# Sink attention with a mixer: the products of two heads beside each other in halves of the TensorE array, and a written order ahead of the branch

## The chip, the cores and the metric

The kernel runs on one core of a Trainium2 chip. The metric is the time of one execution on the device in microseconds (us). The kernel before is given as a median of 3 executions; the profile shows a further execution of it.

## What is computed

Inputs have 4 batches, 8 heads, 768 positions and 64 numbers per head. Attention keeps, for each query, 4 sink keys and a window of the last 128 keys. A low-rank mixer over positions (rank 32) and a two-layer network with a hidden width of 2048 follow, each with a residual sum.

```python
scores = scale * np.matmul(q, k.transpose(0, 1, 3, 2))
keep = is_sink | in_window
scores = np.where(keep, scores, -1000000000.0)
a = np.exp(scores - np.max(scores, axis=-1, keepdims=True))
a = a / (np.sum(a, axis=-1, keepdims=True) + 1e-09)
attn = np.matmul(a, v)                # then x: [4, 768, 512]
h = x.transpose(0, 2, 1) @ U @ V
u = x + h.transpose(0, 2, 1)
out = u + np.maximum(u @ w_ch1, 0.0) @ w_ch2
```

U, V and the two weight matrices arrive as 8-byte floats.

## The kernel before, in words

**Attention.** One head and one half of its queries (three blocks of 128) are a unit. For each block, TensorE makes the scores against 4 sink keys and at most 256 window keys in one bank (line 637 or, in split form, lines 640 and 641). VectorE adds the mask and takes the minimum of the negated scores in one instruction with a second one that reads its accumulator (643). ScalarE makes the exponentials and their sums (648). The unit is then normalised (667 to 691), transposed on TensorE (702), masked into triangles (711 on VectorE, 727 on GpSimd), and multiplied with the values (752); a copy puts the result into `xT`. Batches 0 and 1 (`WHOLE`) do the scores and values in plain 4-byte floats; batches 2 and 3 split each operand into two parts first. A score contracts over 64 numbers: in batches 0 and 1 the lower 64 of the 128 partitions of `q` and `k` hold zeros, which come with the inputs (and from four memsets for the first two heads, lines 1287 and 1288). A value product of batches 0 and 1 has 128 output rows, of which the lower 64 belong to the next block's values and are not used.

**Weights.** Each of the 16 steps of the network (`f`) needs two pieces of 128x512 weights. A piece in 8-byte floats is loaded into `big`, turned into a 4-byte float by the VectorE and ScalarE steps of lines 94 to 103, and split into two parts (lines 462, 469). These are the conversions; there are 32 of them, all in the first third of the execution. Converted weights also go to memory (`wd`) and are fetched from there later.

**Network.** A step on TensorE is 12 products of 384 columns (966 to 968), a ReLU (974) and its remainder `hl` (977), and 9 products of 512 columns (987). Batch 0 runs the 16 steps on both halves of the positions in groups of four: four new steps on one half, the same four on the other, and so on. Attention of batch `b + 1` is placed among the network steps of batch `b`.

**Order.** No loop order is written out. Every operation is a `Step` with a duration, an engine or a choice of engines, and a due time. `Plan.order` places them by these numbers and their dependences, several rounds forwards and backwards, and the program is emitted in the resulting order. So a change of one duration or dependence moves instructions everywhere. Each engine then runs its own instructions strictly in that order and waits at each for what it needs. Ahead of the network and attention stands a short part that loads two limits, builds masks and branches on them (`Masks`, `load_scalars`, lines 1271 to 1303).

## Time and profile before

| what | us |
|---|---|
| median of 3 executions (761.8 to 762.37) | 762.2 |
| the profiled execution | 760.85 |
| its span, first to last instruction | 759.1 |
| TensorE busy | 745.9 (98%) |
| VectorE busy | 459.1 (60%) |
| ScalarE busy | 353.4 (47%) |
| GpSimd busy | 187.9 (25%) |

The span does not hold 1.75 us that lie around it. A record of a matmul in the profile is longer than the time until the next one starts, because the array works on several at once; the busy share of TensorE can therefore stay near 100% while it still has room. A plain 4-byte product stands in the profile as two records.

### The profile page before, as it was taken

To read this page: it belongs to the slowest core of one execution; us is meant where nothing else is said; L and a number is where in the kernel's file an instruction comes from. 1 tells how busy PE (TensorE), PEld (TensorE's weight loads), DVE (VectorE), ACT (ScalarE), POOL (GpSimd) and SP (SyncE) were. 2 spreads that over 40 slices of the span, in tenths; PEclk is the share of its full clock that TensorE was granted. 3 is DMA by queue.
4 is the path that set the end of the run, shared out by engine and by line. 5 is a ranking of instruction groups with operands and counts; after the bars stand their busy time and mean duration, and the time that the engine had idled before them with its cause. 6 is when DMAs were issued, how large, how long until landed. Compare 5 with 4: busy or idle time off the path is not lost.

```text
span 759.1 us, 11690 instructions
## 1 busy us (share of the span) xinstructions
PE 745.9 (98%) x4012; PEld 667.4 (88%) x4012; DVE 459.1 (60%) x1184; ACT 353.4 (47%) x1024; POOL 187.9 (25%) x288
## 2 busy tenths in 40 slices
PE   8999999999999999999999999999999999999997
PEld 6786998888888999999999989899999898989995
DVE  8989779898899586676853176766653131112111
ACT  6997367666676374564551155555542111111110
POOL 4761011223232344424611033522501000000000
PEclk9999999999999999999999999999999999999999
DMA  8898477773876478762586448761266527523752
GB/s 289 277 318 293 180 268 251 264 260 105 280 236 232 147 192 259 232 220 77 168 265 218 166 130 280 233 191 49 69 217 225 210 92 260 186 102 129 257 189 95
DMA packets 46981, 153.90 MB, mean 203 GB/s; under 512 B 5824, under 2 KB 13888, under 8 KB 37440
## 3 DMA queue, kind: packets, MB, share of 16 engines
q1 hardware_dynamic: 46752, 152.86, 60.7%
q8 instruction: 33, 0.54, 0.3%
q14 instruction: 36, 0.29, 0.1%
q10 hardware_dynamic: 160, 0.20, 0.1%
HBM read 123.42 MB, written 29.62 MB: 202 GB/s over the span
## 4 chain that ended last, share of the span: by engine, by line
PE 91%; DVE 5%; ACT 2%; issue 1%; POOL 0%; DMA 0%; POOLq 0%; DVEq 0%
PE bank L987 35%; PE bank L966 12%; PE bank L968 12%; PE bank L967 12%; PE bank L752 6%; PE bank L637 4%; PE bank L702 2%; PE bank L640 2%; PE bank L641 1%; PE bank L866 1%; DVE bank L101 1%; PE bank L1004 1%; ACT p L648 1%; DVE p L469 1%; PE bank L849 1%
## 5 line engine op out<-in xcount | busy, mean ns | idle before, releaser
L987 PE MATMUL bank<-w,hh 128*128 128x512 f32 x768 | 243.4, 398 | 0.0
L977 DVE SCALAR_TENSOR_TENSOR hl<-bank,hh 128x384 fp32r<-128x384 f32 x128 | 70.8, 553 | 189.2 <-ACT hh L974 188.7
L966 PE MATMUL bank<-ul,w 128*128 128x384 f32 x512 | 178.9, 349 | 0.0
L968 PE MATMUL bank<-uh,w 128*128 128x384 f32 x512 | 172.8, 337 | 0.0
L967 PE MATMUL bank<-uh,w 128*128 128x384 f32 x512 | 172.3, 337 | 0.0
L974 ACT ACTIVATE hh<-bank 128x384 fp32r<-128x384 f32 x119 | 58.4, 491 | 220.8 <-PE bank L968 219.9
L987 PEld LDWEIGHTS bank<-w,hh 128*128 128x128 f32 x768 | 139.3, 188 | 19.4
L987 PE MATMUL bank<-w,hl 128*128 128x512 f32 x384 | 152.3, 397 | 0.0
L648 ACT ACTIVATE p<-p,mn 128x260 f32<-128x260 f32 (+1 forms) x192 | 93.3, 487 | 41.0 <-DVE mn L643 40.5
L967 PEld LDWEIGHTS bank<-uh,w 128*128 128x128 f32 x512 | 96.4, 188 | 5.7
L966 PEld LDWEIGHTS bank<-ul,w 128*128 128x128 f32 x512 | 96.2, 188 | 5.7
L968 PEld LDWEIGHTS bank<-uh,w 128*128 128x128 f32 x512 | 96.0, 188 | 0.0
L987 PEld LDWEIGHTS bank<-w,hl 128*128 128x128 f32 x384 | 72.1, 188 | 17.7 <-DVE hl L977 1.1
L643 DVE CUSTOM_DVE_ANT_0 p<-bank,mask 128x260 f32<-128x260 f32 (+1 forms) x192 | 70.9, 400 | 17.6 <-PE bank L641 13.3
L682 POOL TENSOR_TENSOR p<-p,r 128x396 f32<-128x396 f32 x33 | 29.0, 878 | 113.1 <-DVE r L670 95.9
L471 POOL TENSOR_TENSOR ul<-xT,uh 128x384 fp32r<-128x384 f32 x15 | 15.1, 1022 | 122.0 <-ACT uh L462 84.8
L727 POOL TENSOR_SCALAR_AFFINE_SELECT oph<-oph 128x384 f32<-128x384 f32 (+1 forms) x64 | 36.3, 567 | 21.5 <-ACT oph L462 17.7
L471 POOL TENSOR_TENSOR p<-p 128x256 f32<-128x256 f32 (+1 forms) x22 | 19.2, 871 | 81.2 <-ACT p L648 77.7
L752 PEld LDWEIGHTS bank<-oph,vhl 128*128 128x128 f32 x224 | 35.8, 190 | 3.9 <-POOL oph L727 0.6
L752 PE MATMUL bank<-oph,vhl 128*128 128x256 f32 (+1 forms) x224 | 38.9, 303 | 0.0
L648 ACT ACTIVATION_READ_ACCUMULATOR p<-p,mn 128x1 f32 x192 | 36.1, 188 | 0.0
L702 PE MATMUL bank<-ident,p 128*128 128x128 f32 x192 | 33.3, 277 | 1.9 <-ACT p L680 1.5
(178 smaller groups left out, 1079.5 us busy)
## 6 DMA issues: line engine op xcount, KB each, us to landing
w<-wd SPq DMA_DIRECT2D x60, 1024.0 KB, 4.9
big<-in_w_dram SPq DMA_DIRECT2D x32, 512.0 KB, 5.4
wd<-w SPq DMA_DIRECT2D x14, 1024.0 KB, 4.8
big<-xd SPq DMA_DIRECT2D x33, 256.0 KB, 3.1
qkraw<-in_q_dram SPq DMA_DIRECT2D x39, 192.0 KB, 4.3
qkraw<-in_k_dram SPq DMA_DIRECT2D x32, 198.0 KB, 5.6
out_dram<-big SPq DMA_DIRECT2D x24, 256.0 KB, 2.1
v_raw<-in_v_dram SPq DMA_DIRECT2D x16, 192.0 KB, 2.8
```

What stands on the lines that cost most here:

```text
L471: ways["POOL"] = (gps(n), lambda: nc.gpsimd.tensor_tensor(dst(), a(), b(), op), True)
L643: add("DVE", dve(wd), lambda st=st, u=u, lo=lo, wd=wd, qb=qb: nc.vector.tensor_tensor_reduce(p()[:, u, NS + lo:], st()[:, :wd], self.mask[ ...
L648: add("ACT", act(wd) + 0.22, lambda u=u, lo=lo: nc.scalar.activation(p()[:, u, NS + lo:], p()[:, u, NS + lo:], AF.Exp, bias=mn()[:, u:u + ...
L702: nc.tensor.transpose(tr()[:, u * P:(u + 1) * P], p()[:, u, SW + NS:], self.ident)
L727: add("POOL", 0.126 + CH * 0.914e-3, lambda t=t: nc.gpsimd.affine_select(as_(t()[:, :, 1, :]), f32(t()[:, :, 1, :]), [[0, NBLK], [1, P]], ...
L752: nc.tensor.matmul(out, st, f32(mv) if whole else mv, start=part == 0 and i == 0, stop=part == len(t) - 1 and i == len(mms) - 1, skip_grou ...
L966: nc.tensor.matmul(ph()[:, :CH], wh, ul()[:, d, :], start=d == 0, stop=False)
L967: nc.tensor.matmul(ph()[:, :CH], wl, uh()[:, d, :], start=False, stop=False)
L968: nc.tensor.matmul(ph()[:, :CH], wh, uh()[:, d, :], start=False, stop=d == NC - 1)
L974: self.plan.any({"ACT": (act(CH), lambda: nc.scalar.activation(hh(), ph()[:, :CH], AF.Relu)), "DVE": (dve(CH), lambda: nc.vector.tensor_sc ...
L977: add("DVE", dve(CH), lambda: nc.vector.scalar_tensor_tensor(hl(), ph()[:, :CH], 0.0, f32(hh()), ALU.max, ALU.subtract), r=(ph, hh), w=(hl ...
L987: nc.tensor.matmul(acc[k](), a()[:, sl], w()[:, m, :], start=not begin and i == 0 and j == 0, stop=i == n - 1 and j == 2)
```

## The change

In batches 0 and 1, two heads are now one unit. `load_pair` puts the two heads' `q` and `k` into the upper and the lower 64 partitions of one tile, without zeros. For every block of queries, `attend_pair` issues two score products, one per head, on the two halves of the partitions and into two banks. For the values it issues the two heads' products in turn, each with 64 stationary columns, into the upper and the lower 64 rows of one bank, and one copy of 128x384 replaces two of 64x384. The planner's durations for these are `0.105 + wd / 600.0` for two scores of `wd` columns (before `0.005 + wd / 600.0` for one) and 1.25 and 1.50 for two heads' values (before 1.08 and 1.30 for one). A second tile per unit for the exponentials is taken from the ring `qkraw`. Sums and minima share one small tile. The batches 2 and 3 keep their form. The part ahead of the branch is emitted as written, with the distances of `Masks` first and the masks filled ahead of the load of the flag.

```diff
+NSM = 7
+PAIRED = 2
...
-ACC = (0xFFFF, 0xFFFF, 0xFFFF, 0xFFFF)
-WHOLE = {0: (0xFFFF, 0xFFFF), 1: (0xFF, 0xFF)}
...
+def two_heads(x, b, pr):
+
+    return x[b, 2 * pr:2 * pr + 2].rearrange("h d n -> (h d) n")
...
-        kr, qr = (self.kh(), self.qs()) if h % 2 else (self.kl(), self.qkraw())
-        self.put(kr, lambda: (f32(kr()[:, :k1 - k0]), self.k[b, h][:, k0:k1]), (k1 - k0) * 512, t0 - 16)
-        self.put(qr, lambda: (f32(qr()[:, :q1 - q0]), self.q[b, h][:, q0:q1]), (q1 - q0) * 512, t0 - 15)
-        return qr, kr, None, q0, k0
-
-    def scores(self, half, t0, acc, qs, kh, kl, qbase=0, kbase=0):
+        kr, qr = self.kh(), self.qs()
+        self.put(kr, lambda: (f32(kr()[:, :k1 - k0]), two_heads(self.k, b, pr)[:, k0:k1]), (k1 - k0) * 512, t0 - 16)
+        self.put(qr, lambda: (f32(qr()[:, :q1 - q0]), two_heads(self.q, b, pr)[:, q0:q1]), (q1 - q0) * 512, t0 - 15)
+        return qr, kr, q0, k0
+
+    def load_v_pair(self, b, pr, blocks, t0):
+
+        k0, k1 = blocks
+        n = k1 - k0
+        t = self.vhl()
+        flat = lambda: f32(t().rearrange("p n s d -> p (n s d)")[:, :2 * n * D])
+        for i in range(2):
+            self.put(t, lambda i=i: (flat()[:, i * n * D:(i + 1) * n * D].rearrange("p (n d) -> p n d", n=n),
+                                     self.v[b, 2 * pr + i][:, k0:k1, :]), n * 32768, t0 - 8, part=i)
+        return t, flat, k0, n
...
+    def attend_pair(self, b, pr, half, t0, qk, v, xT):
+
         nc, add = self.nc, self.plan.add
-        p, mn, sm = self.p(), self.mn(), self.sm()
+        qr, kr, qbase, kbase = qk
+        wide = lambda: self.pool.tile([P, NB * SW], F32, name="qkraw", bufs=NRAW).rearrange("p (n s) -> p n s", n=NBLK)
+        ps = [self.p(), self.qkraw(wide)]
+        sms = [self.ms(), self.ms()]
+        for u in range(NBLK):
+            qb = half * NBLK + u
+            lo = P if qb == 0 else 0
+            k0 = max(qb - 1, 0) * SW + (NS if qb else 0) - kbase
+            q0 = qb * P - qbase
+            wd = UW - lo
+            sts = [self.bank(), self.bank()]
+
+            def mms(sts=sts, q0=q0, k0=k0, wd=wd):
+                for i, st in enumerate(sts):
+                    rows = slice(i * D, (i + 1) * D)
+                    nc.tensor.matmul(
+                        st()[:, :wd], f32(qr()[rows, q0:q0 + P]), f32(kr()[rows, k0:k0 + wd]), start=True, stop=True)
+            add("PE", 0.105 + wd / 600.0, mms, r=[qr, kr] + [(p, u) for p in ps], w=sts, prio=t0, after=self.gate)
+            for st, p, sm in zip(sts, ps, sms):
+                self.soften(st, p, sm, u, lo, wd, qb, t0)
+        ts = []
+        for i in range(2):
+            self.normalise(b, 2 * pr + i, half, t0 + i, ps[i], sms[i], self.sinks[b])
+            ts += self.transposes(half, t0 + i, ps[i], True, self.opl if i else self.oph)
+        pa = self.bank()
+        t, flat, kb0, n = v
+        mms = []
+        for kb in range(max(half * NBLK - 1, 0), (half + 1) * NBLK):
+            lo = 2 * (kb - half * NBLK) + 1
+            hi = min(lo + 2, 2 * NBLK)
+            lo = max(lo, 0)
+            mms.append((kb, lo, hi, max(kb - half * NBLK, 0)))
+
+        def run():
+            for j, (kb, lo, hi, c0) in enumerate(mms):
+                for i in range(2):
+                    mv = ts[i]().rearrange("p u s j -> p (u s j)")[:, lo * P:hi * P]
+                    at = (i * n + kb - kb0) * D
+                    nc.tensor.matmul(
+                        pa()[i * D:(i + 1) * D, c0 * P:(c0 + hi - lo) * P], flat()[:, at:at + D], f32(mv),
+                        start=j == 0, stop=j == len(mms) - 1, skip_group_check=True)
+        both = [(xT, (half, 0)), (xT, (half, 1))]
+        add("PE", (0.0, 1.25, 1.50)[len(mms) - 2], run, r=ts + [t] + both, w=(pa,), prio=t0)
+        self.copy(CH, lambda: xT()[:, half * CH:(half + 1) * CH], lambda: pa()[:, :CH], psum=True, r=(pa,), w=both, prio=t0)
+
...
+            if b < PAIRED:
+                if h % 2 == 0:
+                    pr = h // 2
+                    qk, v = self.load_pair(b, pr, (0, 1), t0), self.load_v_pair(b, pr, (0, NB), t0)
+                    for half in range(2):
+                        self.attend_pair(b, pr, half, self.t0(16 * b + 2 * (h + half)), qk, v, self.x[b][-1])
+                continue
+            qk = self.prep_qk(b, h, (0, 1), t0)
+            v = self.prep_v(b, h, (0, NB), t0)
             for half in range(2):
-                self.attend(b, h, half, self.t0(16 * b + 2 * h + half), qk, v, self.x[b][-1], whole_v)
+                self.attend(b, h, half, self.t0(16 * b + 2 * h + half), qk, v, self.x[b][-1])
...
+        for pr in range(NPAIR):
+            t0 = self.t0(16 * b + half * H + 2 * pr)
+            qk = self.load_pair(b, pr, (half, half), t0)
+            v = self.load_v_pair(b, pr, (max(half * NBLK - 1, 0), (half + 1) * NBLK), t0)
+            self.attend_pair(b, pr, half, t0, qk, v, self.x[b][pr])
...
-        self.mn, self.sm = ring(NP + 1, [P, NBLK], F32, "mn"), ring(NP + 1, [P, NBLK], F32, "sm")
-        self.rr = ring(3, [P, NBLK], F32, "r")
+        self.ms = ring(NSM, [P, 2 * NBLK], F32, "ms")
+        self.rr = ring(4, [P, NBLK], F32, "r")
...
+    with tc.tile_pool(name="work", bufs=1) as work, tc.tile_pool(name="idle", bufs=1, space=PSUM) as idle, \
+            tc.manual_schedule():
...
+        masks = Masks(nc, sp, work)
         first = []
-        for h, n in enumerate((HALF, DM)):
-            qt, kt = (pre.tile([P, n], F32, name=f"first{h}{x}") for x in "qk")
-            nc.sync.dma_start(kt[0:D, :NBLK * SW], k[0, h][0:D, :NBLK * SW])
-            nc.scalar.dma_start(qt[0:D, :CH], q[0, h][0:D, :CH])
-            nc.vector.memset(qt[D:P, :CH], 0.0)
-            nc.vector.memset(kt[D:P, :NBLK * SW], 0.0)
+        for pr, n in enumerate((HALF, DM)):
+            qt, kt = (pre.tile([P, n], F32, name=f"first{pr}{x}") for x in "qk")
+            nc.sync.dma_start(kt[:, :NBLK * SW], two_heads(k, 0, pr)[:, :NBLK * SW])
+            nc.scalar.dma_start(qt[:, :CH], two_heads(q, 0, pr)[:, :CH])
             first.append((qt, kt))
...
         ns, w, flag = values()
+        masks.fill(ns, w)
         rv = nc.values_load(flag[0:1, 0:1], min_val=0, max_val=1)
-        masks.fill(ns, w)
```

On TensorE, at the start of attention of batch 0, this stands in the program before (`first`, `kl`, `kh` are keys, `qkraw`, `qs` queries, `p` exponentials, `oph`, `opl` their transposes, `vhl` values):

```order
L637 MATMUL bank_165<-kh,qs 128x132
L637 MATMUL bank_166<-kh,qs 128x260
L637 MATMUL bank_167<-kh,qs 128x260
L702 MATMUL bank_168<-ident,p_179 128x128 x3
L752 MATMUL bank_169<-oph,vhl 128x256 x2
L752 MATMUL bank_169<-oph,vhl 128x128
```

And this in the changed program:

```order
L652 MATMUL bank_166<-kh,qs 128x132
L652 MATMUL bank_167<-kh,qs 128x132
L652 MATMUL bank_168<-kh,qs 128x260
L652 MATMUL bank_169<-kh,qs 128x260
L652 MATMUL bank_162<-kh,qs 128x260
L652 MATMUL bank_163<-kh,qs 128x260
L745 MATMUL bank_164<-ident,p_177 128x128 x3
L745 MATMUL bank_165<-ident,qkraw 128x128 x3
L675 MATMUL bank_166<-oph,vhl 64x256
L675 MATMUL bank_166<-opl,vhl 64x256
```

The number of products per head is the same; they now come in twos, from `oph` and `opl` in turn for the values.

On TensorE, where the first attention of batch 1 stands among the network steps of batch 0 (`w`, `ul`, `uh` belong to the network), before:

```order
L968 MATMUL bank_167<-uh,w_173 128x384
L637 MATMUL bank_168<-kl,qkraw 128x132
L637 MATMUL bank_164<-kl,qkraw 128x260
L637 MATMUL bank_166<-kl,qkraw 128x260
L637 MATMUL bank_163<-kl,qkraw 128x260
L637 MATMUL bank_168<-kl,qkraw 128x260
L637 MATMUL bank_164<-kl,qkraw 128x260
L966 MATMUL bank_167<-ul,w_173 128x384
```

And in the changed program:

```order
L1008 MATMUL bank_167<-uh,w_172 128x384
L652 MATMUL bank_169<-kh,qs 128x132
L652 MATMUL bank_168<-kh,qs 128x132
L652 MATMUL bank_166<-kh,qs 128x260
L652 MATMUL bank_162<-kh,qs 128x260
L1006 MATMUL bank_167<-ul,w_172 128x384
L1007 MATMUL bank_167<-uh,w_172 128x384
L1008 MATMUL bank_167<-uh,w_172 128x384
L652 MATMUL bank_169<-kh,qs 128x260
L652 MATMUL bank_168<-kh,qs 128x260
L1006 MATMUL bank_167<-ul,w_172 128x384
```

The twelve scores of a pair of heads are now spread in smaller groups. Between the start of the network of batch 0 and the end of attention of batch 1, the changed program has 17 groups of scores and 8 of values, each with network products or transposes ahead of it and behind it.

On VectorE, around the first remainder `hl` of the network, before (`bank`, `nr` and `w` belong to conversions; a row that writes `w` ends one):

```order
L469 TENSOR_TENSOR w_174<-bank_163,w_174 128x512
L101 SCALAR_TENSOR_TENSOR bank_164<-big_93,nr 128x512
L96 TENSOR_SCALAR nr<-nr 128x512
L102 TENSOR_TENSOR bank_164<-nr,bank_164 128x512
L942 TENSOR_TENSOR xT<-xT,bank_168 128x384
...
L469 TENSOR_TENSOR w_174<-bank_164,w_174 128x512
...
L977 SCALAR_TENSOR_TENSOR hl<-bank_165,hh 128x384
```

And in the changed program:

```order
L474 TENSOR_TENSOR w_170<-bank_167,w_170 128x512
L101 TENSOR_SCALAR nr<-nr 128x512
L106 SCALAR_TENSOR_TENSOR bank_164<-big_107,nr 128x512
L982 TENSOR_TENSOR xT<-xT,bank_165 128x384
...
L474 TENSOR_TENSOR w_172<-bank_164,w_172 128x512
L104 SCALAR_TENSOR_TENSOR nr<-big_109,nr 128x512
L1017 SCALAR_TENSOR_TENSOR hl<-bank_168,hh 128x384
```

Ahead of the first `hl`, the program before ends six conversions (`w_171`, `w_173` and `w_174`, two each), the changed one three (two of `w_170`, one of `w_172`). The other three now stand behind it.

## Rows read from the trace of the kernel before

**Rows 1.** The page: busy share in tenths, 40 slices of 19 us.

```profile
PE   8999999999999999999999999999999999999997
...
DVE  8989779898899586676853176766653131112111
ACT  6997367666676374564551155555542111111110
```

**Rows 2.** Stretches; length, busy time of each engine (instructions), granted clock, DMA share.

```profile
core 0: us, PE busy (x) PEld busy (x) DVE busy (x) ACT busy (x) POOL busy (x), PEclk, DMA share, GB/s
3.40:79.70 76.30, 71.55 (x367) 57.33 (x367) 70.77 (x237) 62.75 (x207) 36.36 (x54) 1.00 0.90 307
79.70:248.00 168.30, 167.00 (x879) 148.55 (x878) 145.21 (x364) 105.64 (x279) 37.35 (x44) 1.00 0.69 230
...
14.80:31.80 17.00, 16.97 (x95) 14.61 (x96) 15.63 (x64) 16.90 (x68) 12.17 (x19) 1.00 0.88 274
...
262.00:753.50 491.50, 490.82 (x2689) 446.09 (x2687) 232.76 (x566) 179.63 (x530) 106.56 (x172) 1.00 0.55 180
```

**Rows 3.** The chain that ended last, 0 to 90 us: start, length.

```profile
16.17 1.10 PE bank L637 x6
...
60.81 0.20 DVE nr L96
61.01 0.62 DVE bank L101
61.65 0.69 DVE bank L102
...
62.54 0.61 DVE nr L99
63.17 0.29 DVE nr L100
63.46 0.60 DVE w L469
...
76.56 0.18 PE bank L966
...
80.80 2.09 PE bank L987 x9
```

**Rows 4.** VectorE in order of time, the first and a later remainder of the network.

```profile
79.69 0.55 DVE L977 SCALAR_TENSOR_TENSOR hl<-bank,hh 128x384 fp32r<-128x384 f32 x1
...
247.98 0.56 DVE L977 SCALAR_TENSOR_TENSOR hl<-bank,hh 128x384 fp32r<-128x384 f32 x1 [0.26 <-ACT hh L974]
```

**Rows 5.** The chain that ended last, 85 to 260 us.

```profile
101.62 2.42 PE bank L637 x12
...
125.79 2.39 PE bank L752 x14
...
219.74 1.84 DVE nr L96
```

**Rows 6.** TensorE in order of time, 196 us.

```profile
195.88 0.34 PE L968 MATMUL bank<-uh,w 128*128 128x384 f32 x1
196.06 0.34 PE L966 MATMUL bank<-ul,w 128*128 128x384 f32 x1
```

**Rows 7.** ScalarE by line and form, 5 to 76 us; count, busy us, mean ns.

```profile
L462 ACT COPY xT<-bank 64x384 f32<-64x384 f32 x14 | 6.6, 468 | 0.2
```

**Rows 8.** All engines in order of time, the start.

```profile
3.42 0.16 DVE L116 SCALAR_TENSOR_TENSOR sc_t<-sc_raw 128x2 f32<-128x2 int32 x1 [0.85 <-DMA sc_raw<-in_limits_dram]
...
4.20 0.29 DVE L145 CAST m_back<-m_rel 128x268 f32<-128x268 int32 x1
...
5.28 2.51 PE L637 MATMUL bank<-first0k,first0q 128*128 128x132 f32 x6 [0.68 <-DVE m_ck L155]
...
6.57 0.29 DVE L643 CUSTOM_DVE_ANT_0 p<-bank,mask 128x132 f32<-128x132 f32 x1 [0.27 <-DVE mask L160]
```

More of the change, by code (lines that the diff above doesn't have):

```diff
@@ L626, in scores @@
+    def scores(self, half, t0, qs, kh, kl, qbase=0, kbase=0):
+        nc, add = self.nc, self.plan.add
+        p, sm = self.p(), self.ms()
         for u in range(NBLK):
@@ L671, in normalise @@
         kept = lambda: p()[:, :, SW:]
         by = lambda: r().unsqueeze(2).broadcast_to([P, NBLK, SW])
-        if acc:
-            u0 = 1 if half == 0 else 0
-            own, past = lambda: p()[:, u0:, SW + NS:], lambda: p()[:, u0:, NS:SW]
-            self.tt((NBLK - u0) * P, own, own, past, ALU.add, w=(p,), prio=t0)
-            def scale():
-                for u in range(NBLK):
-                    nc.scalar.activation(p()[:, u, SW:], p()[:, u, SW:], AF.Copy, scale=r()[:, u:u + 1])
-            self.plan.any({"ACT": (NBLK * 0.3, scale),
-                           "POOL": (0.82, lambda: nc.gpsimd.tensor_tensor(kept(), kept(), by(), ALU.mult), True),
-                           "DVE": (dve(NBLK * SW), lambda: nc.vector.tensor_tensor(kept(), kept(), by(), ALU.mult), True)},
-                          r=(r,), w=(p,), prio=t0)
-        else:
-            self.plan.any({"POOL": (0.82, lambda: nc.gpsimd.tensor_tensor(kept(), kept(), by(), ALU.mult), True),
-                           "DVE": (dve(NBLK * SW), lambda: nc.vector.tensor_tensor(kept(), kept(), by(), ALU.mult), True)},
-                          r=(r,), w=(p,), prio=t0)
+        u0 = 1 if half == 0 else 0
@@ new lines, in normalise, with scale @@
+        own, past = lambda: p()[:, u0:, SW + NS:], lambda: p()[:, u0:, NS:SW]
+        self.tt((NBLK - u0) * P, own, own, past, ALU.add, w=(p,), prio=t0)
+        def scale():
+            for u in range(NBLK):
+                nc.scalar.activation(p()[:, u, SW:], p()[:, u, SW:], AF.Copy, scale=r()[:, u:u + 1])
+        self.plan.any({"ACT": (NBLK * 0.3, scale),
+                       "POOL": (0.82, lambda: nc.gpsimd.tensor_tensor(kept(), kept(), by(), ALU.mult), True),
+                       "DVE": (dve(NBLK * SW), lambda: nc.vector.tensor_tensor(kept(), kept(), by(), ALU.mult), True)},
+                      r=(r,), w=(p,), prio=t0)
@@ L693, in normalise, with transposes @@
                       r=(p,), w=((psink, (half, h)),), prio=t0)
-    def transposes(self, half, t0, p, whole):
+    def transposes(self, half, t0, p, whole, own=None):
         nc, add = self.nc, self.plan.add
         tr = self.bank()
-        res = [self.oph()] if whole else [self.oph(), self.opl()]
+        res = [own()] if whole else [self.oph(), self.opl()]
         def mms():
@@ L764, in values, with attend @@
                 r=(pa, tb), w=((xT, (half, hh)),), prio=t0)
-    def attend(self, b, h, half, t0, qk, v, xT, whole=False):
-        acc = ACC[b] >> (half * H + h) & 1
-        p, sm = self.scores(half, t0, acc, *qk)
-        self.normalise(b, h, half, t0, acc, p, sm, self.sinks[b])
-        t = self.transposes(half, t0, p, whole)
-        self.values(h, half, t0, t, v, xT)
+    def attend(self, b, h, half, t0, qk, v, xT):
+        p, sm = self.scores(half, t0, *qk)
+        self.normalise(b, h, half, t0, p, sm, self.sinks[b])
+        self.values(h, half, t0, self.transposes(half, t0, p, False), v, xT)
     def attention(self, b):
@@ L1119, in run @@
             tiles.append(self.pool.tile([P, NBLK, SW + SW], F32, name=f"p{i}"))
-            nc.gpsimd.memset(tiles[-1][:, :, 0:NS], 0.0)
         with tc.manual_schedule():
@@ L1273, in sink_attention_mixer @@
     ident = sp.tile([P, P], F32, name="ident")
-    with tc.tile_pool(name="work", bufs=1) as work, tc.tile_pool(name="idle", bufs=1, space=PSUM) as idle:
+    with tc.tile_pool(name="work", bufs=1) as work, tc.tile_pool(name="idle", bufs=1, space=PSUM) as idle, \
+            tc.manual_schedule():
         zero = nc.const_aps.tensor(0.0, [P, P], F32)
@@ L1293, in sink_attention_mixer @@
             nc.sync.dma_start(early[-1].bitcast(U16)[:, 1:4 * n + 1], src)
-        masks = Masks(nc, sp, work)
         tri = sp.tile([P, 2, P], F32, name="tri")
```

100 lines of the change are left out of this document (32 added, 68 removed).

## The prediction

> **What bounds the kernel now.** I read the slices of the page first. TensorE is at 8 or 9 tenths throughout, VectorE at 8 and 9 in the first third and then falls to 1 [rows 1]. So I cut the span into stretches [rows 2], at two instructions of VectorE: the first remainder `hl` of the network, at 79.7 us, and the one at 248.0 us that stands just ahead of the end of attention of batch 1 [rows 4]. I call 3.4 to 79.7 us stage A (attention of batch 0), 79.7 to 248 us stage B (network of batch 0, attention of batch 1, most conversions), and what follows stage C.
>
> In stage A VectorE is busy 70.8 of 76.3 us, 92.8%, and between 14.8 and 31.8 us ScalarE 16.9 of 17.0 us [rows 2]. The chain passes through TensorE's scores for a while (16.17 us) and then through conversions on VectorE (from 60.81 us) [rows 3]: three engines take turns as the last one. In stage B TensorE is busy 167.0 of 168.3 us and VectorE 145.2, 86.3% [rows 2]; the chain is TensorE's, apart from a piece near 220 us where an instruction of a conversion took 1.84 us [rows 5] that took 0.20 us at 60.81 us [rows 3]. Stage C is TensorE alone: 490.8 of 491.5 us from 262 to 753.5 us, VectorE under half [rows 2]. The change leaves that work as it is, so what is won ahead of 248 us is kept to the end, and nothing can be won behind it.
>
> **The parts of the change, and what each costs.**
>
> *The start.* VectorE begins the distances at 4.20 us, behind the limits (3.42 us), and its first score at 6.57 us [rows 8]. In the changed order the distances stand ahead of the limits, in time that the four removed memsets and a wait filled. The chain of the limits to the flag stays. TensorE's first score at 5.28 us [rows 8] cannot come earlier, since it needs the flag. What is freed is the stretch from 4.20 us to the filling of the masks, about 1 us, of which the arrival of the scores takes some back: I take -0.5 us, bounds -1 and 0.
>
> *Loads.* A pair's `q` and `k` need as many bytes as one padded head did, so these loads are halved. The DMA share of stage A is 0.90 [rows 2], but the chain there is of engines, not of transfers [rows 3]: nothing is taken for this. If the cover were gone, the transfers would be fewer than now, so the sign is safe. SP's order puts the weights' loads behind fewer loads of heads.
>
> *Copies.* 14 copies of 64x384 to `xT` on ScalarE in stage A took 0.468 us each [rows 7]. A pair needs one copy instead of two, so of 16 copies 8 go, 3.7 us on ScalarE or VectorE. Beside them the merged small tiles and the dropped memsets cost nothing that shows.
>
> *Conversions that move.* One conversion on VectorE is, in the chain, 0.20 + 0.62 + 0.69 + 0.61 + 0.29 + 0.60 = 3.0 us [rows 3]. The changed order has three of them ahead of the first `hl`, the present one six. So 9.0 us of VectorE's work leave stage A and enter stage B. In stage A this shortens the engine that is last at its end: -9.0 us. It could be more, by the copies (-13), if TensorE's freed time lets the engines pack; it could be less (-5), if ScalarE, full from 14.8 us on, keeps the attention at its length and only the end of the stage gets shorter.
>
> *The first weights come later.* The network now starts with one and a half steps' weights. Behind the first `hl`, the other two and a half of the first four steps are five conversions, 15.0 us, with three more `hl` of 0.55 us [rows 4]: 16.6 us of VectorE. In that time TensorE has six half steps of 2.1 us (80.80 us, 9 products of 512 columns, and as much for the 12 of 384 columns between 76.56 us and there, twice over) [rows 3], 12.6 us. TensorE then waits about 4 us that it does not wait now. Queued behind it are all network steps of batch 0.
>
> *TensorE's pairs, in stage B.* One head costs 2.42 us for its six scores (12 records) and 2.39 us for its seven value products [rows 5]; eight heads 38.5 us. No row shows two products in two parts of the array: all rows of before use 128 by 128. Bounds: if they run fully beside each other, 19.3 us remain. A product is two records, so the second head's first record starts beside the first head's second; each group of pairs then ends one record late, 2.42 / 12 to 0.22 us. With 25 groups (17 of scores, 8 of values) that is 5.5 us, 24.8 us in all, 13.7 saved. At the other end a product ends 0.34 us after its start while the next starts after 0.18 us [rows 6]: if the array has to run empty at each of 50 switches, 0.16 to 0.17 us each, 8.5 us more are lost and 5.2 saved. I take 12 us, near the first: in stage B transposes, scores and network products alternate now, and TensorE's busy time has no hole from it (167.0 of 168.3 us [rows 2]). In stage A the same saving does not count by itself, since VectorE and ScalarE are full there.
>
> The Trainium skill speaks against this part: its page "TensorEngine Tiling (Array Packing)", section "Tiling Modes", says that a change of the tiling mode drains TensorE. By that the lower saving, 5.2 us, would hold, and the sum below would be 750 us and not 748. No run of before shows a change of mode.
>
> *Stage B, taken together.* TensorE would need 167.0 - 12 + 4 = 159.0 us. VectorE would be busy 145.2 + 9.0 = 154.2 us, 97% of that. It has not been that full over any long stretch: 92.8% in stage A, 86.3% in B [rows 2]. So TensorE's saving runs into VectorE. I take 94%, a little over stage A because its waits for TensorE's scores get rarer: 164.0 us, -4.3 us. Bounds: 159.0 us (-9.3), and, with the share of today, 178.7 us (+10.4).
>
> **The sum.** 760.85 (the profiled execution) - 0.5 - 9.0 - 4.3 = 747.05 us. The median lies 1.35 us above that execution, so 748.4 us.
>
> **Rivals.**
>
> *TensorE alone bounds stage B.* VectorE packs to 97%, for which its choices of engine speak (ScalarE is busy 105.6 of 168.3 us there [rows 2]): -9.3 instead of -4.3 us, 743.4 us; with the copies in stage A 739.4 us.
>
> *VectorE is as full as now and no fuller.* Every conversion waits for loads, ScalarE and banks as before, and the work that was moved only arrives later: 748.4 + 4.3 + 10.4 = 763.1 us, no change. At 90% stage B is 171.3 us, and the time 755.7 us. For it speaks that instructions of conversions stretch while GpSimd works, as at 219.74 us [rows 5].
>
> *The two heads take turns (slower).* If products in two parts of the array follow each other and every switch empties it, the pairs save nothing in stage B and cost 8.5 us; with the wait of 4 us stage B takes 179.5 us, +11.2. In stage A TensorE, busy 71.6 of 76.3 us [rows 2], stays among the engines that are last, and I leave 5 us of the 9. Sum: 762.2 - 0.5 - 5 + 11.2 = 767.9 us. This decides from the point where the eight heads' products cost 45 us instead of 38.5 (stage B then grows by the 9.5 us that the start and stage A give). For it: the planner orders the program as if they overlapped. Against it: the operands are in different partitions and, for scores, different banks. It is also the case in which the change does not do what it says.
>
> *The pairs overlap, but each switch empties the array.* The saving is 5.2 us, TensorE needs 165.8 us in stage B and bounds it, and the time is 762.2 - 9.5 - 2.5 = 750.2 us. That lies in the band of the forecast below, of which I give it a third.
>
> **How the numbers follow.** A measurement of this kernel can tell about 0.2%, 1.5 us, from no change. Chances: the forecast (745 to 755 us) 0.52; TensorE alone (under 745) 0.17; VectorE between 90% and 86%, still faster (755 to 760.7) 0.13; no change 0.07; slower 0.11, nearly all of it the turns. Faster is then 0.82. The range reaches from 739 us (stage A with the copies, stage B by TensorE) to 761 us, which leaves some 0.03 below it and 0.17 above it. The forecast's own range is 745 to 755 us.
>
> **What the profile of the changed kernel would show.** The start: the first score instruction of VectorE near 6.0 us. Stage A: the first `hl` near 70 us, and five conversions between it and the fifth. Pairs: the second product of a pair starts about 0.22 us after the first and the next pair 0.44 us after it, not 0.88; the 24 score pairs and 8 groups of values of batch 1 take 25 to 28 us of starts on TensorE. Waits: 2 to 6 us of TensorE for conversions within 20 us of the network's start. Stage B: about 164 us, VectorE at 94%. Stage C as now, 505 us from the last remainder of stage B (248.0) to 753.5 us. The prediction is wrong if the pairs start 0.44 us apart, if a gap of 0.17 us stands at each switch and adds up, or if VectorE idles in stage B behind loads of weights.

## The result, and the profile after

The changed kernel takes 752.56 us (median of 4 runs, 752.26 to 754.8), the kernel before, on the same chip, 762.0 us: a ratio of 0.9883, 95% interval 0.987 to 0.9895. The profiled execution took 752.26 us (span 750.5) beside 760.85 (span 759.1), so 8.6 us were won. The forecast was 748.4 us.

The page of the changed kernel, busy share in tenths, 40 slices of 18.8 us:

```profile
PE   7989999999998999999999999999999999999997
...
DVE  7999889798999577667751287675653131112111
ACT  6986475775874445555541164564441111111110
```

Against [rows 1] the tenths of VectorE hardly differ: they are too coarse to show this change. The stretches, cut at the same two remainders `hl` and at the last products (columns as in [rows 2]):

```profile
3.40:69.00 65.60, 56.62 (x365) 38.23 (x365) 61.88 (x216) 53.13 (x182) 33.52 (x54) 1.00 0.67 223
69.00:239.84 170.84, 163.60 (x892) 129.59 (x891) 155.43 (x389) 108.66 (x285) 40.89 (x53) 1.00 0.68 235
239.84:744.93 505.09, 504.55 (x2749) 458.83 (x2747) 235.12 (x562) 178.15 (x509) 117.48 (x197) 1.00 0.54 181
```

Stage A is 65.6 us instead of 76.3, stage B 170.8 instead of 168.3, stage C 505.1. By this cut all of the gain was made in stage A (10.7 us), and stage B gave 2.5 us of it back. The cut itself has moved, since three conversions of 3.0 us now stand behind it; over both stages the gain is 8.1 us. In A VectorE is busy 61.9 us, 94.3%, in B 155.4 us, 91.0%, and in B TensorE has 7.2 us without work, where it had 1.3 [rows 2]. What TensorE waited for there, 69 to 239.84 us (us in total, times, longest):

```profile
PE bank L1027 <- DVE hl L1017: 2.3, 2, 2.1
PE bank L1007 <- DVE w L474: 1.8, 6, 0.3
PE bank L1006 <- ACT w L467: 0.7, 2, 0.4
```

Most of it is the end of a conversion (`w`) or a remainder (`hl`) on VectorE; the third row is a conversion's step on ScalarE. Short waits don't show in this table at all: the record of a product is longer than its distance to the next one, as in [rows 6], and covers them. Summed by the starts of the network's products, whose own distances are 0.18 and 0.23 us, TensorE waited about 10 us in B: 4.2 at 72 to 83 us, 3.7 at 230 to 237 us, the rest mainly at 120 to 128 and 165 to 176 us. In the kernel before the same sum gives no wait. The chain that ended last shows the first of these places:

```profile
69.07 0.47 DVE hl L1017
...
73.53 0.70 DVE bank L106
74.23 0.21 DVE nr L101
...
74.46 0.64 ACT nr L103
...
75.12 0.69 DVE nr L104
75.82 0.60 DVE w L474
...
86.85 2.11 PE bank L1027 x9
...
108.63 1.23 PE bank L675 x12
...
111.29 1.47 PE bank L675 x16
```

From 61.5 to 83.0 us the chain is mostly VectorE's, conversion after conversion, and not TensorE's as at 76.56 to 80.80 us in [rows 3]. Over the whole of stage B it is still TensorE's for the larger part: the network's products make 49.9% of it, scores and values 12.5%, and four lines of VectorE (conversions and `hl`: L104, L474, L106, L1017) 15.6%. The last two lines are the pairs' values: 1.23 and 1.47 us for both heads, where one head took 2.39 us for both halves [rows 5].

TensorE in order of time, 98 us, around a group of two score products among network products, and the first values of a pair:

```profile
98.17 0.34 PE L1007 MATMUL bank<-uh,w 128*128 128x384 f32 x1
98.35 0.33 PE L1008 MATMUL bank<-uh,w 128*128 128x384 f32 x1
98.61 0.71 PE L652 MATMUL bank<-kh,qs 64*128 64x260 f32 x4
99.25 0.44 PE L1006 MATMUL bank<-ul,w 128*128 128x384 f32 x1
99.53 0.34 PE L1007 MATMUL bank<-uh,w 128*128 128x384 f32 x1
...
108.56 0.43 PE L675 MATMUL bank<-oph,vhl 128*64 128x256 f32 x1
108.57 0.43 PE L675 MATMUL bank<-opl,vhl 128*64 128x256 f32 x1
108.83 0.38 PE L675 MATMUL bank<-oph,vhl 128*64 128x256 f32 x1
```

The same group with a shorter window, the first records of a group of eight products (186 us), and network products behind a wait for a conversion (76 us):

```profile
98.61 0.49 PE L652 MATMUL bank<-kh,qs 64*128 64x260 f32 x2
...
186.32 0.38 PE L652 MATMUL bank<-kh,qs 64*128 64x132 f32 x2
...
76.47 0.44 PE L1007 MATMUL bank<-uh,w 128*128 128x384 f32 x1 [0.33 <-DVE w L474]
76.75 0.34 PE L1008 MATMUL bank<-uh,w 128*128 128x384 f32 x1
```

The values of two heads start 0.01 us apart: they do run beside each other. So do the scores: two records of 0.48 us stand within 0.49 us, and from start to start they are 0.01 us apart. The next two follow 0.32 us later and the network 0.31 us behind those (0.64 us in all), while in the middle of longer groups two records of 260 columns follow two others after 0.22 us. So a group of two scores pays 0.20 us inside itself. It also starts 0.26 us behind its neighbour where the neighbours' distance is 0.18, and the second product behind it comes 0.28 us after the first (99.25, 99.53): about 0.09 us ahead of a group and 0.10 behind it, 0.19 us. (The same 0.28 us stands behind a plain wait, 76.47 to 76.75 us, so that part belongs to any start after a pause.) Together that is 0.40 us for a group of scores, with 2 or with 8 products in it. For values it is 0.34 us: 1.23 + 0.19 us where six steps of 0.22 or 0.11 us make 1.08. Two scores that stand alone so cost 0.64 + 0.19 = 0.83 us instead of 0.88. The Trainium skill, page "TensorEngine Tiling (Array Packing)", section "Tiling Modes", says that a change of mode drains TensorE; the trace agrees, and gives the size.

The start, VectorE and TensorE in order of time:

```profile
4.30 0.16 DVE L121 SCALAR_TENSOR_TENSOR sc_t<-sc_raw 128x2 f32<-128x2 int32 x1 [1.52 <-DMA sc_raw<-in_limits_dram]
...
7.54 0.21 DVE L101 TENSOR_SCALAR nr<-nr 128x192 bf16<-128x192 bf16 x1 [1.24 <-ACT nr L100]
7.67 0.29 DVE L704 CUSTOM_DVE_ANT_0 p<-bank,mask 128x132 f32<-128x132 f32 x1
```

Against [rows 8] the limits landed 0.88 us later, and the first score on VectorE comes 3.37 us behind them instead of 3.15, at 7.67 us instead of 6.57: the distances are out of the way, but a conversion's instruction (L101) now stands ahead of the score and waits 1.24 us.

### The profile page after: what moved, and what is told of

Its sections match the earlier page's. It is cut to its first block, busy times and chain, and to the rows that moved or that the text cites. A ratio compares the mean times of both kernels' runs of the same rounds, so it can differ in the third digit from the quotient of the medians.

```text
span 750.5 us, 11587 instructions
## 1 busy us (share of the span) xinstructions
PE 727.3 (97%) x4012; PEld 629.2 (84%) x4012; DVE 454.3 (61%) x1168; ACT 341.4 (45%) x977; POOL 194.0 (26%) x316
## 4 chain that ended last, share of the span: by engine, by line
PE 84%; DVE 11%; ACT 1%; issue 1%; DMA 1%; POOL 0%; SPq 0%; DVEq 0%; ACTq 0%
PE bank L1027 33%; PE bank L1006 12%; PE bank L1007 11%; PE bank L1008 11%; PE bank L793 3%; PE bank L745 2%; PE bank L652 2%; PE bank L675 2%; DVE nr L104 2%; PE bank L695 2%; PE bank L696 2%; DVE w L474 1%; DVE bank L106 1%; PE bank L906 1%; DVE p L704 1%
## 5 line engine op out<-in xcount | busy, mean ns | idle before, releaser
L1027 PE MATMUL bank<-w,hh 128*128 128x512 f32 x768 | 246.2, 402 | 1.2 <-ACT hh L1014 0.6
L1017 DVE SCALAR_TENSOR_TENSOR hl<-bank,hh 128x384 fp32r<-128x384 f32 x128 | 70.9, 554 | 186.9 <-ACT hh L1014 186.1
L707 ACT ACTIVATE p<-p,ms 128x132 f32<-128x132 f32 (+1 forms) x144 | 69.9, 486 | 33.4 <-DVE ms L704 32.9
L704 DVE CUSTOM_DVE_ANT_0 p<-bank,mask 128x132 f32<-128x132 f32 (+1 forms) x144 | 54.3, 401 | 13.3 <-PE bank L696 10.8
L476 POOL TENSOR_TENSOR p<-p 128x256 f32<-128x256 f32 (+1 forms) x26 | 21.7, 836 | 131.0 <-ACT p L707 130.3
L467 ACT COPY tb<-bank 64x384 f32<-64x384 f32 x31 | 14.7, 474 | 40.0 <-PE bank L793 40.0
L729 POOL TENSOR_TENSOR p<-p,r 128x396 f32<-128x396 f32 x27 | 24.2, 898 | 32.4 <-DVE r L718 26.0
L474 DVE TENSOR_TENSOR xT<-bank,tb 64x384 f32<-64x384 f32 x32 | 17.5, 548 | 23.1 <-ACT tb L467 22.8
L770 POOL TENSOR_SCALAR_AFFINE_SELECT oph<-oph 128x384 fp32r<-128x384 f32 (+1 forms) x48 | 27.4, 572 | 12.8 <-ACT oph L467 10.2
L745 PE MATMUL bank<-ident,p 128*128 128x128 f32 x144 | 24.9, 278 | 3.4 <-POOL p L729 2.2
L770 POOL TENSOR_SCALAR_AFFINE_SELECT opl<-opl 128x384 fp32r<-128x384 f32 (+1 forms) x48 | 26.1, 544 | 7.4 <-ACT opl L467 4.1
```

The costliest lines, as they stand in the source:

```text
L474: ways = {"DVE": (dve(n), lambda: nc.vector.tensor_tensor(dst(), a(), b(), op), pool)}
L476: ways["POOL"] = (gps(n), lambda: nc.gpsimd.tensor_tensor(dst(), a(), b(), op), True)
L704: add("DVE", dve(wd), lambda: nc.vector.tensor_tensor_reduce(p()[:, u, NS + lo:], st()[:, :wd], self.mask[:, min(qb, 2), lo:], -0.125, 3.0 ...
L707: add("ACT", act(wd) + 0.22, lambda: nc.scalar.activation(p()[:, u, NS + lo:], p()[:, u, NS + lo:], AF.Exp, bias=sm()[:, u:u + 1], scale=-1.0,
L745: nc.tensor.transpose(tr()[:, u * P:(u + 1) * P], p()[:, u, SW + NS:], self.ident)
L770: add("POOL", 0.126 + CH * 0.914e-3, lambda t=t: nc.gpsimd.affine_select(as_(t()[:, :, 1, :]), f32(t()[:, :, 1, :]), [[0, NBLK], [1, P]], ...
```

## The experiments

The experiments ran on chips where the kernel before took 762.33 to 762.37 us; ratios are to it. The times below are compared with the 752.56 us of the change. The first three keep the planner's order of the steps behind the branch; in the others the planner, given other durations or steps, also orders anew. What that alone can do is seen at the three that change only its numbers or its groups (measured durations, attention later, larger groups): 0.5 to 9.6 us more. In all paired kernels that were ordered anew the first remainder `hl` stands at 73.0 to 78.4 us instead of 69.0. The cut between A and B moves with the order, so the sum of both stages is the safer thing to compare.

**The start undone.** The changed kernel with the order of before ahead of the branch:

```diff
-    with tc.tile_pool(name="work", bufs=1) as work, tc.tile_pool(name="idle", bufs=1, space=PSUM) as idle, \
-            tc.manual_schedule():
+    with tc.tile_pool(name="work", bufs=1) as work, tc.tile_pool(name="idle", bufs=1, space=PSUM) as idle:
...
-        masks = Masks(nc, sp, work)
         first = []
...
+        masks = Masks(nc, sp, work)
...
-        masks.fill(ns, w)
         rv = nc.values_load(flag[0:1, 0:1], min_val=0, max_val=1)
+        masks.fill(ns, w)
```

> The changed kernel with the part ahead of the branch as it was before (loads first, distances behind them, masks filled behind the load of the flag, order left to the framework); attention and network unchanged. Theory that the new start costs time (the limits arrive later behind nothing that was moved, and VectorE's first instruction behind the branch waits for a load of U): the first score on VectorE stays near 7.5 us because that wait is in the part that is kept, and the time is 752.0 to 752.8 us. Theory that the new start by itself delays the limits: the limits arrive near 3.4 us again, the first score stands near 6.6 to 7.0 us, and the time is 751.5 us. Theory of the prediction (the new start saves 0.5 us): 753.0 us.

Measured 753.39 us (752.54 to 755.87), ratio 0.9892 [0.9873, 0.9912]. The limits are late here too:

```profile
4.49 0.16 DVE L121 SCALAR_TENSOR_TENSOR sc_t<-sc_raw 128x2 f32<-128x2 int32 x1 [4.49 <-DMA sc_raw<-in_limits_dram]
```

The first score stands at 8.16 us, 3.67 behind them. So the order of the start did not delay the limits, and it saves 0.30 us behind them in the changed kernel (3.37).

**The start alone.** The same edit the other way round, in the kernel before:

> The kernel before with only the part ahead of the branch in the new written order (its four memsets kept, behind the distances). If the written order saves the 0.5 us of the prediction: 761.5 us, VectorE's first score near 6.0 us. If it delays the limits: first score near 7 us, 762.5 to 763 us.

Measured 762.38 us, ratio 0.9998 [0.9988, 1.0008]. In its trace:

```profile
4.15 0.39 DVE L1290 MEMSET first1k<- 64x396 f32 x1
4.57 0.16 DVE L116 SCALAR_TENSOR_TENSOR sc_t<-sc_raw 128x2 f32<-128x2 int32 x1
```

The limits landed at 3.42 us, but the four memsets, now behind the distances, hold VectorE until 4.54 us. The first score stands at 7.14 us, 2.57 behind the first instruction on the limits (L116) instead of 3.15. The 0.58 us are there, near the forecast's 0.5, and the memsets, which the changed kernel has not, take more than that back. Over all runs the landing goes with the kernel: 3.40 to 3.45 us in the kernel before and its three variants, 4.24 to 4.58 us in the changed one and its nine. So it is not scatter: something in the changed kernel other than the written order costs the limits 0.8 us or more. What it is was not tested; the first loads of keys and queries, which now fill 128 partitions instead of 64, are one candidate.

**The values of two heads in turn.** Same planner order, only the loops inside a group of values exchanged:

```diff
-            for j, (kb, lo, hi, c0) in enumerate(mms):
-                for i in range(2):
+            for i in range(2):
+                for j, (kb, lo, hi, c0) in enumerate(mms):
```

> The changed kernel with the order of all engines kept, but in each group of value products first all of one head's and then all of the other's, so that only two records at the border can run beside each other. A group should grow on TensorE from 1.23 and 1.47 us to about 2.0 and 2.4 us, which in stage B is 6.5 to 8 us of TensorE. Theory that VectorE's conversions bound stage B and TensorE has room: +1 to +4 us (754 to 757 us). Theory that TensorE bounds stage B and every microsecond of it counts: +6.5 to +8 us or more (759 to 761 us). If the two heads never ran beside each other: no change in the groups or in the time.

Measured 757.94 us, ratio 0.9942 [0.9922, 0.9962]. The chain of this kernel, same groups as above:

```profile
110.73 1.71 PE bank L675 x11
113.87 2.17 PE bank L675 x14
```

Issued in turn, a group takes 1.71 and 2.17 us instead of 1.23 and 1.47 (one and two of the 12 and 16 records run beside others and are not on the chain). The overlap of the two halves of the array is real and worth 0.48 and 0.70 us a group. The 16 groups of both batches add 9 us to TensorE, and the time grows by 5.4 us: between the two theories.

**Lighter conversions, in the changed kernel** (the sign step left out: VectorE's 0.69 us once per conversion, 35 times up to the end of attention of batch 1):

```diff
         for i, ((ways, r, w), c) in enumerate(zip(steps, cost)):
+            if i == 3:
+                continue
```

> The changed kernel without the step of each conversion that puts the sign back (one VectorE instruction of 0.60 to 0.70 us for each of 32 pieces and of U and V; weights lose their sign, and the output with them). It takes about 22 us off VectorE ahead of the end of stage B, four of them in stage A. Theory that VectorE bounds stage B: 12 us or more of waits and fill go, 739 to 744 us. Theory that TensorE's own groups and switches bound it: only stage A gets shorter, 748 to 751 us.

Measured 744.56 us, ratio 0.9769 [0.9746, 0.9791], 8 us less. Its stage B:

```profile
73.67:232.20 158.53, 158.21 (x886) 129.67 (x886) 138.38 (x356) 97.03 (x262) 39.06 (x53) 1.00 0.70 241
```

With VectorE at 138.4 us of 158.5 (87%) TensorE has 0.3 us without work, and summed by their starts the network's products do not wait (10 us in the change): this is about what stage B costs when TensorE alone bounds it, 12.3 us less than in the change. Part of that is the cut: five conversions instead of three stand ahead of the first `hl` here, and stage A is 4.7 us longer (70.3 us). Both stages together take 7.6 us less.

**The same in the kernel before:**

> The kernel before without the step of each conversion that puts the sign back, as in the run of the changed kernel (the output loses the signs of the weights). Theory that VectorE bounds stage B only since the change, and TensorE did before: only stage A gets shorter, 1 to 5 us less, 757 to 761 us, so less than the 8 us that the changed kernel won by it. If VectorE bounded stage B before as well: 8 us or more less, 754 us or below.

Measured 763.37 us, ratio 1.0011 [0.9999, 1.0024]. The same work taken from VectorE was worth nothing before the change and 8 us behind it.

**Heavier conversions** (the sign step done twice), in the changed kernel and in the kernel before:

```diff
-            self.plan.any({e: (c if e == "DVE" else gps(n) if e == "POOL" else act(n) + 0.09, fn, e != "ACT" and not (x and i == 6))
-                           for e, fn in ways.items()}, r=r, w=(w,), prio=prio)
+            for _ in range(2 if i == 3 else 1):
+                self.plan.any({e: (c if e == "DVE" else gps(n) if e == "POOL" else act(n) + 0.09, fn, e != "ACT" and not (x and i == 6))
+                               for e, fn in ways.items()}, r=r, w=(w,), prio=prio)
```

> The changed kernel; each conversion does its sign step (35 of 0.69 us ahead of the end of attention of batch 1) twice, 24 us more VectorE work there. Theory (VectorE bounds this stretch, and is at most some 92% busy in it): 217 + 24 us of work take 262 us instead of 236.4, so the time grows by about 25 us, 774 to 781 us. Rival (TensorE and its waits bound it, VectorE only at places): VectorE's idle 19 us take up most of it, +4 to +10 us, 756 to 763 us.

> The kernel before with the same doubled step. Theory (TensorE bounded this stretch before, VectorE was 88% busy over it): the idle 28.6 us of VectorE take up a part; 216 + 24 us at 92% are 261 us instead of 244.6, so +10 to +17 us, 772 to 779 us, less than the changed kernel gains in the same experiment, and the two end together. Rival (VectorE bounded it before as well): +24 us or more, 786 us.

Measured 785.44 us (ratio 1.0302 [1.0278, 1.0325]), +32.9 us, and 780.05 us (1.0245 [1.0221, 1.0269]), +17.7 us. Both rivals fall, and both times lie above the theory's ranges too: the changed kernel paid more than the 25 us expected, and the two do not end together. It pays nearly twice as much for the same work, and ends above the other. Two stretches of its trace (columns as before, the granted clock third from the end):

```profile
40.00:60.00 20.00, 14.80 (x98) 9.60 (x98) 17.13 (x50) 16.44 (x59) 8.05 (x13) 0.83 0.43 136
60.00:80.00 20.00, 19.70 (x100) 14.80 (x101) 19.58 (x38) 12.17 (x25) 4.42 (x4) 1.00 0.65 232
```

In the first stretch, where TensorE is idle for 5.2 us, the granted clock is 0.83, a mean over its two levels of 2.4 and 1.2 GHz; in the second, where it is idle for 0.3 us, it is 1.00. Some of the 32.9 us is therefore TensorE at its lower level, which stands nowhere in stages A and B of the changed kernel (1.00 above). How much was not tested apart. Nor do the lighter and heavier conversions tell VectorE's load from the length of a conversion's chain, since both change by the same instruction.

**Only the scores in pairs**, each head's values again by 128 stationary columns into a bank of its own, with two copies:

```diff
-        pa = self.bank()
+        pas = [self.bank(), self.bank()]
...
-                    at = (i * n + kb - kb0) * D
+                    at = (i * n + kb - kb0 - i) * D
...
-                        pa()[i * D:(i + 1) * D, c0 * P:(c0 + hi - lo) * P], flat()[:, at:at + D], f32(mv),
+                        pa()[:, c0 * P:(c0 + hi - lo) * P], flat()[:, at:at + P], f32(mv),
...
-        add("PE", (0.0, 1.25, 1.50)[len(mms) - 2], run, r=ts + [t] + both, w=(pa,), prio=t0)
+            add("PE", (0.0, 1.08, 1.30)[len(mms) - 2], run, r=[ts[i], t] + mine, w=(pa,), prio=t0)
```

> The changed kernel with the values of two heads no longer beside each other: each head multiplies with 128 stationary columns into its own bank, and a copy of 64x384 per head follows, as before. The scores stay paired. In stage B TensorE's groups of values go from 1.23 and 1.47 us (and 0.19 us of a switch) for two heads back to 2.18 and 2.62 us, 6.9 us in all, and 8 copies of 0.47 us come back in each of the two stages. If the scores' pairs save little by themselves because each small group is paid with a switch: 757 to 760 us. If the scores carry half of what was won: 755 to 756 us.

Measured 764.76 us, ratio 1.0033 [1.002, 1.0046]: outside the expected range. The values of a pair are back at this (chain):

```profile
110.05 2.17 PE bank L675 x12
```

In this order the scores' pairs alone win no time: two products that stand alone cost 0.83 us instead of 0.88, as read above. The gain hangs on the values' pairs (1.23 instead of 2.17 us) and their single copy, which were not tested apart from each other.

**The planner's durations as measured, and the attention of batch 1 later.** `0.30 + wd / 600.0`, 1.42 and 1.66 in place of `0.105 + wd / 600.0`, 1.25 and 1.50; and, in another kernel, `BESIDE` with the first pair (8, 2.75) instead of (6, 2.5):

> The changed kernel with the planner told what a pair costs in the trace, its switches included: 0.30 + wd / 600 for two scores (not 0.105 +), 1.42 and 1.66 for two heads' values (not 1.25 and 1.50). If the order suffers because the planner takes pairs for cheaper than they are: 749 to 751 us. If what is lost is VectorE's load, which no price of TensorE changes: 751.5 to 754 us.

> The changed kernel with attention of batch 1 let in from network step 8 on and one head every 2.75 steps (before from step 6, every 2.5), so that VectorE is free for the conversions for longer. Theory that the waits for conversions among the first attention of batch 1 cost 3 us or more of the loss: 748 to 750 us. Theory that the total load of VectorE in stage B counts, wherever it stands: 751.5 to 754 us.

Measured 755.1 us (ratio 0.9902 [0.988, 0.9925]) and 753.08 us (0.9875 [0.9852, 0.9897]). The first is above both its ranges: truer durations don't help, and cost 2.5 us (for a lone pair of scores even these give 0.73 us, against 0.83 read above). The second is in the range of the load: in this one shift it did not matter when VectorE's work comes.

**Larger groups, and a higher price of VectorE.** The pairs of two query blocks in one group; and `PRICE` with 5.0 instead of 3.0 for VectorE:

```diff
-        for u in range(NBLK):
+        for us in ((0, 1), (2,)):
```

```diff
-PRICE = {"DVE": 3.0, "ACT": 1.5, "POOL": 1.5}
+PRICE = {"DVE": 5.0, "ACT": 1.5, "POOL": 1.5}
```

> The changed kernel; the pairs of the first two query blocks of a half are issued as one group, so TensorE changes between groups of scores and other work 21 times instead of 26. Theory (VectorE bounds): no change, 751 to 754.5 us. Rival (the switches of TensorE, 0.19 us each, and what waits at them, cost the time): 748 to 751 us.

> The changed kernel; the planner's price of VectorE's time in the choice of an engine is 5.0 instead of 3.0, which moves some copies and conversion steps to ScalarE and GpSimd. Theory (VectorE's work bounds the stretch): if some 5 to 10 us leave VectorE, the time falls by 3 to 8 us, 744 to 750 us. Rival (VectorE's idle time is waiting for ScalarE and GpSimd in the middle of conversions): slower engines for single steps lengthen the chains and give it back, 752 to 760 us.

Measured 762.12 us (ratio 1.0002 [0.9985, 1.0018]) and 767.57 us (1.0074 [1.0051, 1.0096]). Both are worse than both theories said. With larger groups the engines' work is nearly the same (table below), but stages A and B together take 8.6 us more, and all of it stands in stage A (75.0 us instead of 65.6, with three conversions ahead of the first `hl` in both): why the engines wait more for each other there was not settled. With the higher price, 38 instructions left VectorE ahead of the end of attention of batch 1 and its busy time stayed at 217 us. VectorE by line and form in stages A and B; count, busy us, mean ns, first the changed kernel:

```profile
L104 DVE SCALAR_TENSOR_TENSOR nr<-big,nr 128x512 uint16<-128x512 uint16 x32 | 22.6, 705 | 0.9
L106 DVE SCALAR_TENSOR_TENSOR bank<-big,nr 128x512 f32<-128x512 uint32 x32 | 22.3, 698 | 0.8
L107 DVE TENSOR_TENSOR bank<-nr,bank 128x512 f32<-128x512 bf16 x32 | 22.1, 690 | 0.2
...
L105 DVE TENSOR_SCALAR nr<-nr 128x512 uint16<-128x512 uint16 x32 | 10.0, 313 | 0.3
L101 DVE TENSOR_SCALAR nr<-nr 128x512 bf16<-128x512 bf16 x32 | 9.5, 295 | 0.0
```

and the same lines of the kernel with the higher price:

```profile
L106 DVE SCALAR_TENSOR_TENSOR bank<-big,nr 128x512 f32<-128x512 uint32 x32 | 24.9, 779 | 1.0
L104 DVE SCALAR_TENSOR_TENSOR nr<-big,nr 128x512 uint16<-128x512 uint16 x32 | 24.4, 762 | 1.4
L107 DVE TENSOR_TENSOR bank<-nr,bank 128x512 f32<-128x512 bf16 x32 | 22.1, 689 | 0.4
...
L105 DVE TENSOR_SCALAR nr<-nr 128x512 uint16<-128x512 uint16 x32 | 14.5, 452 | 0.2
L101 DVE TENSOR_SCALAR nr<-nr 128x512 bf16<-128x512 bf16 x32 | 12.6, 393 | 0.1
```

GpSimd is busy 96.6 us here over the two stages and 74.4 us in the changed kernel. VectorE's instructions that read from SBUF alone got longer (313 to 452, 295 to 393, 705 to 762, and L106, which writes a bank, 698 to 779 ns), 12.0 us together; L107, which reads one operand from a bank, did not (690 and 689). Single instructions of this kernel tie it to GpSimd: where GpSimd is idle, L101, L105 and L106 take 286, 283 and 698 ns on the mean, and where it works for more than 60% of the instruction 972, 776 and 1356 ns; L107 takes 690 and 688. What was given to GpSimd came back as longer instructions on VectorE.

**All kernels together.** Stages A and B as one stretch, from 3.40 us to the remainder that stands at 247.98 us in [rows 4], in us; the shares are worked out from the columns:

| kernel | time | stretch | TensorE busy | VectorE busy | VectorE's share |
|---|---|---|---|---|---|
| before | 762.0 | 244.6 | 238.5 | 216.0 | 88.3% |
| changed | 752.6 | 236.4 | 220.2 | 217.3 | 91.9% |
| start undone | 753.4 | 236.3 | 220.3 | 217.9 | 92.2% |
| start alone | 762.4 | 246.6 | 238.5 | 217.5 | 88.2% |
| values in turn | 757.9 | 241.9 | 229.5 | 218.1 | 90.2% |
| light, changed | 744.6 | 228.8 | 216.5 | 203.0 | 88.7% |
| light, before | 763.4 | 246.6 | 237.5 | 195.7 | 79.4% |
| measured durations | 755.1 | 238.1 | 220.5 | 216.2 | 90.8% |
| attention later | 753.1 | 235.0 | 216.7 | 213.9 | 91.0% |
| scores only | 764.8 | 245.2 | 234.5 | 221.3 | 90.3% |
| heavy, changed | 785.4 | 269.0 | 232.7 | 239.9 | 89.2% |
| heavy, before | 780.1 | 266.3 | 248.1 | 242.7 | 91.1% |
| two blocks a group | 762.1 | 245.0 | 222.3 | 218.0 | 89.0% |
| VectorE dear | 767.6 | 250.4 | 229.9 | 217.0 | 86.7% |

No kernel keeps VectorE over 92.2% busy in that stretch. (In "attention later" 2.5 us more stand behind the cut than in the changed kernel, so its stretch is too short by about that.)

## Why the prediction came out as it did

**The start**, -0.5 us: not seen at the end. Behind the first instruction on the limits the edit saves 0.58 us when made alone and 0.30 in the changed kernel, where L101 waits. But the limits land 0.88 us later, so the first score came at 7.67 us and not near 6.0. The prediction left that chain as it was; what delays it stays open. Undoing the edit costs at most 0.8 us, within the runs' scatter.

**Stage A**, 3.4 us to the first `hl` at 69.0 us: -10.7 us, -9.0 taken. The first `hl` was expected near 70 us, and five conversions end between it and the fifth `hl` (90.13 us), as forecast. What came beyond the three moved conversions, 1.7 us, lies between the -9.0 taken and the bound of -13 with the copies; that it was the copies was argued and not tested apart. It also hangs on this one order: with three conversions ahead of it as well, the first `hl` stands at 78.4 us with larger groups. The loads cost nothing that shows in the stage: the DMA share fell from 0.90 to 0.67.

**TensorE's pairs**, 12 us saved in stage B: the size came near, the terms it was built from did not. From their starts, the 25 groups of batch 1 took 24.1 us, 28.8 with the 0.19 around each, where eight heads took 38.5: 9.7 us saved, 2.3 too few. The prediction took 5.5 us for a second product that starts one record late in every group; the starts 0.01 us apart show that there is none, in scores or values. It took under 2 us for the switches (13.7 less 12); at 0.40 us a group of scores and 0.34 a group of values they cost 9.5. That these two errors nearly cancel is luck. The rival in which each switch empties the array had 0.33 us a group, close to that, and its 750.2 us was nearer to the result; its saving of 5.2 us was too small because it counted the late product as well. A gap at each switch that adds up was one of the prediction's signs of being wrong, and it came. The heads don't take turns.

**Stage B taken together** is the step that failed, as the term "I take 94%": 164.0 us was taken and 170.8 measured. VectorE's work was sized rightly, 155.4 us beside 154.2. Its share was 91.0%, and that alone makes 155.4 / 0.91 = 170.8 instead of 155.4 / 0.94 = 165.3 us, 5.5 of the 6.8 us; the 1.2 us of work are the rest. On TensorE's side the same stands as about 10 us of waits, mostly for conversions and remainders, where 4 were taken: the 4.2 us at the network's start were foreseen, those at 120, 165 and 230 us were not. A share of 94% is not out of reach in itself, since stage A of the changed kernel has 94.3%; it was not reached over B. The rival with VectorE at 90% (755.7 us) lay nearer here than the forecast.

The mechanism of stage B held. That the conversions now end last at places in B, and hardly did before, is shown by the lighter conversions (8.0 us less and TensorE's 10 us of waits gone in the changed kernel, nothing in the one before) and by the heavier ones (+32.9 and +17.7 us). But VectorE alone is no full account: 9 us on TensorE cost 5.4 us as well, and the lighter kernel stops at TensorE's own 158.5 us. With two engines at 96% and 91%, and conversions that pass through ScalarE in their middle, each loses time to the other.

**The sum.** Against 747.05 us for the profiled execution: stage A 1.7 us better (with the start's 0.5 us, which the cut at 3.40 us holds: 1.2), stage B 6.8 us worse, stage C 0.4 us better, 752.25 us; it took 752.26. The time lies in the forecast's range of 745 to 755 us because that range is wide enough for the 6.8 us that stage B missed, less what the other stages gave; as an account of stage B the forecast was too good.

## What to carry to other kernels

When work is taken from the engine that bounds a stage, the next engine's share of that stage says how much is left to win, and a share above the highest that a stretch of that length shows should not be assumed for it, even where a shorter one reaches it (94.3% in stage A, 91.0% in stage B): here three points of it were 5.5 us, beside 8.6 us won. Products that share the array are worth pairing where many follow each other; two small ones between others lose their gain to the switches. A planner's order can move the time by more than an edit does, so an edit is best tested in an order that is held fixed.

## What was not expected of the hardware

A group of products in another shape of the array costs 0.34 us (values) or 0.40 us (scores) above its products' own pace, 0.09 ahead of it, 0.10 behind it and the rest inside, whether 2 or 8 products stand in it. Two products in halves of the array's rows start 0.01 us apart. Two chains of 64 stationary columns run wholly beside each other when they are issued alternately (0.01 us apart), and partly even when one head's products are all issued ahead of the other's (1.71 us, between 1.23 and 2.17). VectorE's instructions that read SBUF alone took up to 3.4 times as long where GpSimd worked beside them (L101: 972 instead of 286 ns). The Trainium skill, page "GPSIMD Engine Reference", section "1. Specifications", says that GpSimd shares its SBUF interfaces with VectorE and collides with instructions in a two-port mode or with two SBUF inputs; the lines above agree: L104 and L106, with two SBUF inputs, grew, and L107, with one beside a bank, did not. L101 and L105 have one input and grew as well; their mode stands in no row.
